# FNet with a squared-ReLU layer, first sequence: other places for the sums of w_out, another engine for the column's folds, pieces repacked

## The chip, the cores and the metric

The kernel runs on one core of a Trainium2 chip. The metric is the device time of one execution in microseconds (us); the median of three runs of the kernel before is 1900.97 us (1900.57 to 1902.41). The engines are called PE (TensorE), DVE (VectorE), ACT (ScalarE), POOL (GpSimd) and SP (SyncE, which here only issues DMAs). Each engine works through its own list of instructions in order, and waits on semaphores for the others.

## The reference

Eight sequences of 3008 rows by 256 columns go through a two-dimensional Fourier transform, of which the real part is kept; the 24064 rows that come out go through two dense layers with a squared ReLU between them.

```python
X = np.fft.fft(x, axis=1)
X = np.fft.fft(X, axis=2)
attn_out = X.real                      # (8, 3008, 256), float32
h = attn_out.reshape(24064, 256) @ w_in      # w_in (256, 2048)
out = np.maximum(h, 0.0) ** 2 @ w_out        # w_out (2048, 256)
```

## The kernel before

**Data.** Everything is fp32. The transform along the rows is done with tables of cosines and sines after the rows of a sequence have been folded onto each other; its two results, `Pt` and `Qt`, hold half of the frequencies of one sequence. The transform along the columns is merged into w_in, which gives `G1` and `G2`.

**Steps.** A sequence b has 6 blocks of up to 252 frequencies, and each block 8 steps j (two slices of 128 of the 2048 hidden features each), so 48 steps for a sequence and 384 in all, numbered i. A step begins with its front (L975): products `hP` and `hQ` into two PSUM buffers, then on DVE `he` (two instructions, L988) and `g` (L990, L991); then ACT does ReLU and square on `g` (L995, L998) and POOL the sums `s` (L1010 to L1012 in even steps, L1020 to L1027 in odd ones). The products with w_out are made for two steps together, with fewer products than usual, from sums of `g` and sums of blocks of w_out (`wsum`): an odd step i does `first_half` (12 products F) for steps i-3 and i-2, the even step after it `second_half` (8 products S). After the fourth pair of a block, `gather` adds the results up: `upper`, `lower`, `joins`, with j = 2 and 3 of the next block. Only the first block (steps 0 to 7) uses `plain` products (L1067, four of 504 columns for a step), since `wsum` isn't there yet.

**Order.** It is written out by hand. Up to step 9 the fronts are cut into halves ("f8b" is the product of the second half of front 8, "d8b" its DVE part), and a list of names, ORDER (L1342), gives the order of everything: conversion of the weights (TS, PW, H, PR), "rl" and "sq" for ReLU and square, "bk6" for the plain products of step 6, "sum8" for the sums of w_out, "fe" and "gE" for a small product and its copy. From step 10 (PLAIN) a loop (L1460) sets the order.

**Sums of w_out.** `sum_wout` (L374) handles one of four groups of SUMS for one half of the columns: ACT copies one or two blocks of w_out into a PSUM buffer, DVE makes 3 to 6 sums or differences from the copy and a block in SBUF, some of them in place. `sums_at` spreads the eight calls over steps 8 to 14. A plain product of a step must come before its slice of w_out is overwritten.

**Pieces.** While one sequence goes through its steps, the next one is folded and transformed, in pieces beside the steps. `fold_later` (L571) makes them: R(t) adds and subtracts the rows of a tile t (ACT copy into PSUM, then DVE `fs` and `fd`, L584 and L585), C(t) folds its columns (two ACT copies into PSUM, two DVE instructions `sc`), `both` splits parities, `order` reverses rows, `even`, `odd` and `twice_...` are later stages. The tiles are called 0, 1, TWO, TWO+1, av, aw, bv, bw. `dft_ops` (L686) makes the pieces "beside", whose products stand between those with w_out: `even` and `odd`, 8 for a sequence. The first sequence has 4 more for one column of all later sequences; that column comes in through small DMAs into `xe` (`load_column`), ACT doubles it (`scale_columns`), and `fold_columns` (L454) folds it in some 20 tiny instructions. `part_table` rearranges tables on ACT.

`ahead(b)` (L1178) puts the pieces of sequence b in line, each with a weight in us. `pieces` (L1320) takes up to two at each step while a budget allows; `piece_beside` is run between the second and the third product. Steps with j = 2 and 3 have hardly a share (SHARE, FIRST).

**Buffers.** The scratch of R, C and the others (`spare`) and of the pieces "beside" comes from the same two PSUM buffers, tag "h", as `hP` and `hQ`: what reads a scratch holds back a front. A buffer freed first is given out first. The two PSUM buffers "d" hold `S1`, `S2` and the small products "pe". `xt`, a tile of x, has three SBUF buffers: R(t) of one tile issues the load of the tile three places later in LATER (L185).

Of the kernel before, what the change touches and what calls it, by code (L numbers as in the profile page):

```python
# [15 lines left out]
P = 128  # L16
R = 32
# [67 lines left out]
def kernel(  # L85
# [99 lines left out]
    LATER = [(b, t) for b in range(1, B) for t in (TWO, TWO + 1, 0, *range(ODD0, NL), 1)]  # L185
# [188 lines left out]
    def sum_wout(qs, shared):  # L374

        ps, held = spare(slice(0, P)), {}
        for i, d in enumerate(shared):
            held[d] = ps[:, i * D:(i + 1) * D].rearrange("p (q h) -> p q h", q=2)  # L380
            nc.scalar.copy(held[d], A(*d)[:, qs])
        for u, v, op, to in SUMS[shared]:
# [71 lines left out]
    def fold_columns():  # L454
# [12 lines left out]
        def begin():  # L467
            s = hp.tile([P, 2, NL, NE], F32, name="es", tag="es", bufs=1)
            tt(out=s, in0=xe[:, 0::2], in1=xe[:, 1::2], op=ALU.add)
            for kp in range(2):  # L470
                tt(out=we[:, :, kp], in0=s[:, 0], in1=s[:, 1], op=ALU.subtract if kp else ALU.add)
# [5 lines left out]
        def copy_even():  # L477
            nc.scalar.copy(a, we[r, first, 0])

        def even():  # L480
            butterfly(we[r, first, 0], we[r, other, 0], a)

        def odd():
            for i, u in enumerate((other, first)):
                tt(out=m[:, 3 * i:3 * i + 3], in0=we[r, u, 1], in1=turned(SIN + i, u), op=ALU.mult)
            for u in (first, other):
                tt(out=we[r, u, 1], in0=we[r, u, 1], in1=turned(COS, u), op=ALU.mult)
            tt(out=we[r, both, 1], in0=we[r, both, 1], in1=m, op=ALU.add)

        def copy_pairs():  # L490
# [3 lines left out]
            nc.scalar.copy(pair, we[r, v, 1])  # L494

        def twice_even():
            butterfly(we[r, 2:3, 0], we[r, 4:5, 0], one)
            for i, u in enumerate((5, 7)):
                mix(out=we[r, u, 0], in0=we[r, u, 0], scalar=by(BY_AB, COS), in1=f[:, i], op0=ALU.mult, op1=ALU.add)

        def twice_odd():
            butterfly(we[r, v, 1], we[r, w, 1], pair)

        return [(0.8, begin), (0.3, order), (0.0, copy_even), (1.0, odd), (0.5, even), (0.0, copy_pairs),
                (0.9, twice_even), (0.5, twice_odd)]
# [65 lines left out]
    def fold_later(b):  # L571
# [5 lines left out]
        def rows_of(t):  # L577
            r = rows(t)

            def f():  # L580
# [4 lines left out]
                tt(out=fd[t][r], in0=v[r, 0::3], in1=p, op=SUB)  # L585
                load_later(LATER.index((b, t)) + NX)

            return 1.3, f
# [89 lines left out]
        R, C, both = rows_of, columns_of, parities_of  # L678
        one = [R(TWO), R(TWO + 1), C(TWO), R(0), C(TWO + 1), both(TWO, TWO + 1), R(av), C(0), order(TWO + 1), C(av),
# [6 lines left out]
    def dft_ops(b):  # L686
# [8 lines left out]
        def group(kp, which):  # L695
# [86 lines left out]
            def join_2():  # L782
                a, ps = st["b"], st["ps"]
                st["c"] = held_w() if both_in else hp.tile([P, NC[0][3]], F32, name="dc2", tag="dc2", bufs=2)[0:n, 0:n0]
# [274 lines left out]
    def second_half(q, n, s, hook=None):  # L1059

        if q == 0:
            open_banks(("S0", "S1", "S2"))
        run((("S0", 0, 8, s[:, 2]), ("S0", 1, (0, 1), s[:, 4]), ("S0", 2, (0, 2), s[:, 8]), ("S1", 0, (1, 0), s[:, 6]),
             ("S1", 1, 11, s[:, 10]), ("S2", 0, 7, s[:, 7]), ("S2", 1, (1, 3), s[:, 5]), ("S1", 2, 10, s[:, 3])),
# [113 lines left out]
    def ahead(b):  # L1178
        (_, start), *groups = dft_ops(b)
        tables = [(0.0, lambda tab=tab, t=t: part_table(tab, t)) for t in (TWO, ODD0) for tab in (cosT, sinT)]  # L1180
        if b == 1:
            early = [(0.0, start), (0.0, take_turn), (0.5, make_turn)]
            middle = [(0.0, scale_columns)] + fold_columns() + tables + dft_ops(None)
        else:
            early, middle = [], []
            groups = [(0.0, start)] + groups
        one, two = fold_later(b)
        return early + one + middle + two + groups
# [120 lines left out]
    FIRST = (1.6, 2.6, 0.2, 0.2, 0.9, 1.9, 1.6, 1.9)  # L1309

    ROOM = (1.6, 2.4, 0.0, 0.0, 1.0, 1.8, 1.6, 1.8)
# [3 lines left out]

    def free_pieces():
        while side and not side[0][0]:
            side.pop(0)[1]()

    def pieces():  # L1320
# [3 lines left out]
        room, count = ROOM[i % NJ] if i >= per else 2.8, 2  # L1324
        while side and count:
            t, f = side[0]
            if f in beside or not t or t > room or spent + t / 2 > 0:
                return
# [248 lines left out]
```

## Time and profile before

| What | Value |
|---|---|
| Median of three runs | 1900.97 us |
| The profiled execution, its own time | 1901.05 us |
| Its span, first to last instruction | 1899.3 us |
| Granted clock of PE, mean | 0.997 |
| PE busy | 1868.8 us, 98% of the span |
| DVE busy | 1478.6 us, 78% |
| POOL busy | 1450.8 us, 76% |
| ACT busy | 1083.0 us, 57% |
| Chain of waits | PE 86%, DVE 10%, ACT 2% |

The page's shares are means over the whole. The first sequence takes the first 302.58 us (the front of step 48 begins then), the next ones some 227 us each; 1.75 us lie outside the span. The idle time of an engine in the groups of instructions stands behind the bar, with what ended it.

### The profile page before, as it was taken

The page shows a single profiled execution, that of the slowest core. Times are in us where ns is not written, and L with a number is a line of the kernel's source. Part 1 is how long each engine was busy: PE and PEld are TensorE (multiplying, and loading weights), DVE is VectorE, ACT ScalarE, POOL GpSimd, SP SyncE. Part 2 cuts the span into 40 slices and gives each one's busy share as a digit, 9 for nine tenths or more (in the row PEclk, how much of TensorE's full clock was granted, in tenths as well). Part 3 has the DMA queues.
Part 4 walks back from the last instruction along what each step waited for, and adds up shares of the span by engine and source line. Part 5 has one row for each costly group of instructions (what it writes and reads, how often), then busy time and mean ns, then how long its engine had stood idle before and what let it go on. Part 6 is the DMA issues. An engine that isn't in the chain of part 4 may idle for free.

```text
span 1899.3 us, 34013 instructions
## 1 busy us (share of the span) xinstructions
PE 1868.8 (98%) x11408; PEld 1755.3 (92%) x11408; DVE 1478.6 (78%) x3507; ACT 1083.0 (57%) x1612; POOL 1450.8 (76%) x2115
## 2 busy tenths in 40 slices
PE   9999999999999999999999999999999999999998
PEld 7678889999999999999999999999999999999997
DVE  8688877888778877888778887788877888766665
ACT  5865655666456654656555574566645656445453
POOL 4367667887788887878778887788778878787886
PEclk9999999999999999999999999999999999999999
DMA  6431101110011000111011110111001100000000
GB/s 196 116 43 32 40 14 42 48 34 15 20 45 51 23 20 20 51 40 29 23 32 31 45 31 15 32 45 48 15 15 45 39 14 19 16 22 15 20 20 23
DMA packets 151310, 68.46 MB, mean 36 GB/s; under 512 B 131143, under 2 KB 142881, under 8 KB 151136
## 3 DMA queue, kind: packets, MB, share of 16 engines
q1 hardware_dynamic: 150590, 65.74, 13.8%
q8 instruction: 91, 1.49, 0.3%
q14 instruction: 83, 0.68, 0.1%
q0 software_dynamic: 416, 0.43, 0.1%
q10 hardware_dynamic: 130, 0.12, 0.0%
HBM read 41.54 MB, written 24.69 MB: 35 GB/s over the span
## 4 chain that ended last, share of the span: by engine, by line
PE 86%; DVE 10%; ACT 2%; issue 1%; POOL 0%; DMA 0%; SPq 0%; DVEq 0%; ACTq 0%; POOLq 0%
PE F L1045 31%; PE S L1045 19%; PE hP L984 15%; PE hQ L984 15%; DVE he L988 2%; PE pd L837 1%; PE pd L714 1%; DVE g L990 1%; DVE g L991 1%; PE mA L1074 1%; PE mB L1074 1%; PE pd L811 1%; PE pg L344 1%; ACT sp L644 1%; PE ph L955 0%
## 5 line engine op out<-in xcount | busy, mean ns | idle before, releaser
L995 ACT ACTIVATE g<-g 128x1008 f32<-128x1008 f32 (+1 forms) x384 | 399.4, 1040 | 313.7 <-DVE g L991 306.0
L988 DVE SCALAR_TENSOR_TENSOR he<-ew,gE,hP 128x252 f32<-128x252 f32 (+1 forms) x748 | 321.2, 470 | 295.9 <-PE hP L984 295.7
L998 ACT ACTIVATE g<-g 128x1008 f32<-128x1008 f32 (+1 forms) x384 | 399.3, 1040 | 12.0
L984 PE MATMUL hP<-Pt,G 128*128 128x252 f32 (+1 forms) x1496 | 380.1, 377 | 8.0 <-DVE w L646 2.9
L984 PE MATMUL hQ<-Qt,G 128*128 128x252 f32 (+3 forms) x1496 | 380.3, 377 | 5.0 <-DVE Pt L749 1.0
L1045 PE MATMUL F<-s,wsum 128*128 128x168 f32 (+1 forms) x1504 | 337.5, 306 | 0.0
L1020 POOL TENSOR_TENSOR s<-g 128x168 f32<-128x168 f32 (+1 forms) x188 | 101.8, 542 | 299.0 <-ACT g L998 294.6
L984 PEld LDWEIGHTS hQ<-Qt,G 128*128 128x128 f32 (+1 forms) x1496 | 280.2, 190 | 48.1 <-ACT g L995 4.2
L1045 PE MATMUL S<-s,wsum 128*128 128x168 f32 (+1 forms) x1504 | 305.7, 305 | 0.0
L1045 PE MATMUL F<-g,wout 128*128 128x168 f32 (+1 forms) x1504 | 305.7, 305 | 0.0
L984 PEld LDWEIGHTS hP<-Pt,G 128*128 128x128 f32 x1496 | 265.2, 190 | 29.7 <-ACT sp L631 4.3
L990 DVE TENSOR_TENSOR g<-he,hQ 128x504 f32<-128x504 f32 (+1 forms) x374 | 253.2, 677 | 49.8 <-PE hQ L984 6.2
L1045 PE MATMUL S<-s,wout 128*128 128x168 f32 (+1 forms) x1504 | 281.2, 306 | 0.1
L1045 PE MATMUL F<-g,wsum 128*128 128x168 f32 (+1 forms) x1504 | 275.0, 305 | 0.0
L1045 PEld LDWEIGHTS S<-s,wsum 128*128 128x128 f32 x1504 | 249.5, 190 | 8.2
L991 DVE TENSOR_TENSOR g<-he,hQ 128x504 f32<-128x504 f32 (+1 forms) x374 | 250.5, 670 | 0.0
L1045 PEld LDWEIGHTS F<-s,wsum 128*128 128x128 f32 x1504 | 248.8, 190 | 0.3 <-issue 0.2
L1045 PEld LDWEIGHTS F<-g,wsum 128*128 128x128 f32 x1504 | 240.6, 190 | 8.1
L1045 PEld LDWEIGHTS F<-g,wout 128*128 128x128 f32 x1504 | 240.6, 190 | 0.0
L1045 PEld LDWEIGHTS S<-s,wout 128*128 128x128 f32 x1504 | 232.1, 190 | 0.7 <-POOL s L1027 0.3
L1026 POOL TENSOR_TENSOR s<-s 128x336 f32<-128x336 f32 (+1 forms) x188 | 168.6, 897 | 14.7
L1023 POOL TENSOR_TENSOR s<-s 128x336 f32<-128x336 f32 (+1 forms) x188 | 168.5, 896 | 14.7
(227 smaller groups left out, 2498.5 us busy)
## 6 DMA issues: line engine op xcount, KB each, us to landing
out_dram<-os SPq DMA_DIRECT2D x376, 56.0 KB
xt<-in_x_dram SPq DMA_DIRECT2D x39, 384.0 KB
xt<-in_x_dram SPq DMA_DIRECT2D x63, 128.0 KB
ew<-e_dram SPq DMA_DIRECT2D x39, 126.0 KB
out_dram<-os SPq DMA_DIRECT2D x288, 7.0 KB
raw<-in_moe_w_in_dram SPq DMA_DIRECT2D x16, 256.0 KB
raw<-in_moe_w_out_dram SPq DMA_DIRECT2D x16, 256.0 KB
xt<-in_x_dram SPq DMA_DIRECT2D x2, 512.0 KB
```

Of the source, the lines that this page charges most:

```text
L344: nc.tensor.matmul(pg, tab[:, i], win[j][:, i], start=i == 0, stop=i == 1)
L984: nc.tensor.matmul(to[:, h, 0:n], w[:, fs], v[:, ks], start=h == 0, stop=True, skip_group_check=True)
L988: nc.vector.scalar_tensor_tensor(out=t[:, h, 0:n], in0=window[b, k0][:, 0:n], scalar=gE[:, fc:fc + 1], in1=hP[:, h, 0:n], op0=ALU.mult, op ...
L990: tt(out=g[:, :, 0:n], in0=t[:, :, 0:n], in1=hQ[:, :, 0:n], op=ALU.add)
L991: tt(out=g[:, :, n:2 * n][:, :, ::-1], in0=t[:, :, 0:n], in1=hQ[:, :, 0:n], op=ALU.subtract)
L995: act(g[:, :, 0:2 * n], g[:, :, 0:2 * n], AF.Relu)
L998: act(g[:, :, 0:2 * n], g[:, :, 0:2 * n], AF.Square)
L1020: gt(out=s[:, 11], in0=b2[:, 0], in1=b1[:, 0], op=SUB)
L1023: gt(out=s[:, 4:6], in0=s[:, 4:6], in1=s[:, 10:11].to_broadcast([P, 2, tb]), op=SUB)
L1026: gt(out=s[:, 6:9:2], in0=s[:, 2:4], in1=s[:, 6:8], op=ADD)
L1045: nc.tensor.matmul(acc[nm][:, slot, 0:tb], w, v, start=q == 0 and nm not in begun, stop=q == NJ // 2 - 1, skip_group_check=True)
L1074: nc.tensor.matmul(acc[nm][:, 0:2 * n], wout[:, j, h, c], g[:, c, 0:2 * n], start=j == c == 0, stop=j == NJ - 1 and c == 1)
```

## The change

1. ORDER is new from "sq4" on. The sums of w_out are no longer one item: "sc" copies a group on ACT into a PSUM buffer "d" (before: "h"), "su" does the DVE part. Groups of the first half (a) stand among steps 4 to 8, those of the second half (b) in steps 8 to 11.
2. The plain products bk6 stand between fronts 8 and 9 (before: behind both halves of front 9), bk7 stands before front 10 (before: behind it).
3. In the first sequence `fd` of R(t) is made on POOL from SBUF; its weight goes from 1.3 to 0.7.
4. The folds of the column go from DVE to POOL, with weights of about 0.1, and are woven between other pieces; multiply-adds are split in two.
5. The pieces of the first sequence have another order (R(1) is the fourth R, where it was the last) and another packer, `first_pieces`, with a room for each j and none for j = 2 and 3. A piece "beside" can now share a step with a piece that holds a scratch. Tile 1 is loaded fourth instead of last.
6. In `second_half` the third product of S1 comes ahead of the two of S2, in all sequences.

```diff
-    LATER = [(b, t) for b in range(1, B) for t in (TWO, TWO + 1, 0, *range(ODD0, NL), 1)]
+    LATER = [(b, t) for b in range(1, B)
+             for t in (TWO, TWO + 1, 0, *(() if b > 1 else (1,)), *range(ODD0, NL), *((1,) if b > 1 else ()))]
...
-    def sum_wout(qs, shared):
-        ps, held = spare(slice(0, P)), {}
-        for i, d in enumerate(shared):
+    shared_w = {}
+    def copy_wout(k, h):
+        ps, held, qs = psd.tile([P, 2 * D], F32, name="sw", tag="d"), {}, slice(2 * h, 2 * h + 2)
+        for i, d in enumerate(list(SUMS)[k]):
             held[d] = ps[:, i * D:(i + 1) * D].rearrange("p (q h) -> p q h", q=2)
             nc.scalar.copy(held[d], A(*d)[:, qs])
-        for u, v, op, to in SUMS[shared]:
+        shared_w[k, h] = held
+    def sum_wout(k, h):
+        held, qs = shared_w.pop((k, h)), slice(2 * h, 2 * h + 2)
+        for u, v, op, to in list(SUMS.values())[k]:
...
         def begin():
+            scale_columns()
             s = hp.tile([P, 2, NL, NE], F32, name="es", tag="es", bufs=1)
-            tt(out=s, in0=xe[:, 0::2], in1=xe[:, 1::2], op=ALU.add)
+            gt(out=s, in0=xe[:, 0::2], in1=xe[:, 1::2], op=ADD)
...
-        return [(0.8, begin), (0.3, order), (0.0, copy_even), (1.0, odd), (0.5, even), (0.0, copy_pairs),
-                (0.9, twice_even), (0.5, twice_odd)]
+        return [(0.1, begin), (0.3, order), (0.1, odd), (0.1, even), (0.1, odd_sums), (0.1, twice_even), (0.1, twice_odd)]
...
-                tt(out=fd[t][r], in0=v[r, 0::3], in1=p, op=SUB)
+                if b == 1:
+                    gt(out=fd[t][r], in0=v[r, 0::3], in1=v[r, 1:3], op=SUB)
+                else:
+                    tt(out=fd[t][r], in0=v[r, 0::3], in1=p, op=SUB)
...
+        if b == 1:
+            one = [R(TWO), R(TWO + 1), C(TWO), R(0), C(TWO + 1), both(TWO, TWO + 1), R(1), C(0), order(TWO + 1), C(1),
+                   R(av), both(0, 1), even((TWO, TWO + 1)), odd(TWO, TWO + 1, BY_TWO)]
+            two = [C(av), R(aw), R(bv), C(aw), both(av, aw), C(bv), order(aw), R(bw), even((av, aw)), odd(av, aw, BY_AC),
+                   C(bw), both(bv, bw), order(bv), even((bv, bw)), odd(bv, bw, BY_BD)]
...
-             ("S1", 1, 11, s[:, 10]), ("S2", 0, 7, s[:, 7]), ("S2", 1, (1, 3), s[:, 5]), ("S1", 2, 10, s[:, 3])),
+             ("S1", 1, 11, s[:, 10]), ("S1", 2, 10, s[:, 3]), ("S2", 0, 7, s[:, 7]), ("S2", 1, (1, 3), s[:, 5])),
...
+        head = [(0.0, start), (0.2, take_turn), (0.5, make_turn)] + one[:9]
+        return (head + woven(one[9:] + two[:3], fold_columns(), 1) + tables
+                + woven(two[3:], dft_ops(None) + groups[0::2], 1) + groups[1::2])
...
+    CAPACITY = (1.8, 2.9, 0.0, 0.0, 1.2, 2.2, 1.8, 2.2)
+    def first_pieces(j):
+        nonlocal spent
+        room, hook = CAPACITY[j], None
+        while side:
+            t, f = side[0]
+            if spent + t / 2 > 0 or t > room + (0.6 if f in beside else 0.3) or f in beside and (hook or late):
+                break
+            side.pop(0)
+            if not t:
+                late.append(f)
+                continue
+            spent, room = spent + t, room - t
+            if f in beside:
+                hook = (2, f)
+            else:
+                f()
+        return hook
...
-        'gE6 PRw4 d6b sq5 fe7 pgC7 gE7 TSw5 bk4 TSw6 PWw5 restQ GC7 d6a spl PWw6 Hw5 f7b PRw5 f7a TSw7 bk5 Hw6 '
-        'PWw7 d7b PRw6 rl6 d7a sq6 f8b Hw7 f8a rl7 d8a sq7 PRw7 d8b sum8 rl8 f9a sq8 hi8 f9b d9a cm8 bk6 '
-        'd9b rl9 sum9 sq9 hi9 cm9 '
+        'gE5 PRw3 pgD6 d5b sq3 f5a GC6 H7 bk3 GD6 rl4 TSw4 PR7 PWw4 d5a pgD7 restP rl5 fe6 Hw4 f6b GD7 sq4 sc0a f6a '
+        'su0a gE6 PRw4 d6b sq5 fe7 pgC7 gE7 TSw5 bk4 TSw6 PWw5 restQ GC7 d6a spl PWw6 Hw5 f7b sc1a PRw5 f7a su1a TSw7 '
+        'bk5 Hw6 PWw7 d7b PRw6 rl6 d7a sq6 f8b Hw7 sc2a f8a rl7 su2a d8b sq7 PRw7 d8a sc3a sc1b bk6 rl8 su3a hi8 su1b '
+        'f9a sq8 f9b d9a cm8 sc2b d9b sc0b rl9 hi9 su2b sq9 bk7 cm9 '
...
-            if i < NJ + 7:
-                sums_at(i)
+            if i == PLAIN:
+                sum_wout(0, 1)
+                copy_wout(3, 1)
+            elif i == PLAIN + 1:
+                sum_wout(3, 1)
...
-        if i == PLAIN:
-            back_at(NJ - 1)
-        elif at >= NJ and at < len(steps):
+        if at >= NJ and at < len(steps):
```

## The prediction

> **What bounds the kernel now.** I read the page's busy shares first, then each engine's busy time by stretches, then what PE waited for, then PE's timeline where it idles.
>
> ```profile
> PE 1868.8 (98%) x11408; PEld 1755.3 (92%) x11408; DVE 1478.6 (78%) x3507; ACT 1083.0 (57%) x1612; POOL 1450.8 (76%) x2115
> ```
>
> PE is the bound over the span, so only PE's idle, slow or waiting time can be won. Stretches (length, then busy time of PE, weight loads, DVE, ACT, POOL) tell where it lies:
>
> ```profile
> 115.13:132.62 17.49, 15.58 (x90) 13.54 (x90) 16.14 (x40) 12.26 (x24) 12.11 (x19) 1.00 0.48 73
> 176.30:225.69 49.39, 45.96 (x283) 41.35 (x282) 41.43 (x101) 29.00 (x50) 34.09 (x50) 1.00 0.17 42
> 302.58:529.39 226.81, 226.18 (x1410) 216.07 (x1409) 181.96 (x428) 131.12 (x194) 180.44 (x264) 1.00 0.12 32
> ```
>
> The second sequence (last row) has PE full; the first has not, and between fronts 13 and 16 (first row) DVE is busier than PE. In steady steps the fronts are 5.12 us (odd) and 3.98 us (even) apart in the timeline; a piece "beside" adds 0.75. From front 10 (100.12) to front 48 (302.58) that makes 172.9, less 0.6 for the six shorter fronts, plus 12 x 0.75: 181.3 of 202.5 us. 21 us are lost there, some 0.14 a piece of it unavoidable, as in the second sequence. Who held PE:
>
> ```profile
> PE hP L984 <- DVE fd L585: 1.9, 4, 0.8
> PE hP L984 <- DVE w L615: 1.9, 1, 1.9
> PE hP L984 <- DVE sc L600: 0.9, 1, 0.9
> ```
>
> DVE's pieces, reading a scratch in a PSUM buffer that the next front needs. Ahead of front 10:
>
> ```profile
> 90.98 0.69 PE L955 MATMUL ph<-Pt,G 128*128 128x252 f32 x2 [2.63 <-DVE g L973]
> 92.97 1.21 PE L955 MATMUL ph<-Pt,G 128*128 128x252 f32 x2 [0.76 <-DVE wout L384]
> 96.50 1.88 PE L1074 MATMUL mB<-g,wout 128*128 128x504 f32 x2
> 99.28 1.01 PE L1074 MATMUL mB<-g,wout 128*128 128x504 f32 x2
> ...
> 92.00:94.00 2.00, 1.24 (x4) 0.86 (x4) 1.97 (x6) 1.11 (x2) 0.78 (x1) 0.50 0.36 3
> ```
>
> Two gaps, 3.4 us, and behind the first the granted clock is 0.50 to 98.7, so the same product takes 1.88 instead of 1.01: another 2.9. So about 27 us, 1.4%, are there to be won, all before 303 us.
>
> **Part by part, against the profiled execution's 1901.05** (the median of the runs shown is 0.08 lower). Work of PE is only moved.
>
> *1. ORDER, sums and plain products (73 to 115 us).* bk6 (four products, 3.4) fills the gap ahead of front 9: 3.4 and the 2.9 of slow clock could come back. But DVE pays. Thirteen more of the sums (0.41 each, starting 0.34 apart: 4.4 us) stand ahead of front 10, and they wait for ACT, whose copies (0.37) queue behind sq4 (ends 76.07) and the conversions. So su0a runs from 76.9 to 79.0 where DVE had idled; the small product fe7 now needs su0a's PSUM buffer (the order of instructions with their waits shows it) and goes from 76.7 to 79.0, with PE's queue behind it: 2.3 lost. su1a waits for sc1a behind a conversion (2.1) on ACT: TSw7 moves from 82.7 to about 87.3, and with it front 8 from 86.5 to 89.7. bk6 then ends at 95.4, bk7 at 100.5, front 10 begins there (before: 100.12), but bk7's 3.4 no longer follow. DVE enters front 10 at 103.0 (before 101.2), with 9 sums to come instead of 22. Carried on: front 13 at 113.5 instead of 115.13. **Gain 1.6.**
>
> *2. Fewer DVE pieces (fronts 13 to 16).* DVE's instructions in these steps go from 6.2, 5.7, 4.8 to 4.4, 3.8, 4.6 (`fd` gone: eight of 0.677 in all; the last sums gone). PE then loses 1.3 instead of 3.3: **gain 2.0**, front 16 at 129.0 instead of 132.62. POOL pays for `fd`: the row at L1209 is the same operation on the same x tile, 1.30 us. Hidden in POOL's waits for squares (L1020: 39.5 us in 16 waits), one in two steps.
>
> *3. Loads (16 to 19).* R(1) moves from step 32 to step 15. Its tile's load is issued on SP behind the `xe` DMAs, which take SP 0.44 to 0.5 each: before, the first load behind them left at 128.2, and such a load landed at 131.3 to 131.9. SP's queue is hardly earlier now (its stores still wait for `os`, 112.3 instead of 112.7). So ACT's copy in R(1), wanted at 127, waits to about 131, with relu and square of front 15 behind it, and `hQ` of front 16 (free when `fs` is done, 132.6) comes 2.75 late. Then scale_columns, moved from step 21 to 17, waits on ACT for the last `xe` DMA (about 141; 0.95). **Loss 3.1.** Without it R(1) would cost nothing.
>
> *4. POOL's lag (19 to 25).* A pair of steps lasts 9.1 and POOL's sums take 8.0 of it. Steps 13 to 23 add seven `fd` (9.1) and the column's fifteen instructions. POOL has no row for those; its smallest of this kind are 0.54 (128x168) and 0.41 (the shorter L1213), its memsets 0.10, DVE's on these shapes 0.16 uncontended: 2.4 to 8.1 us, not below nothing, since they are added to POOL. I take 3.5 (0.23 each, nearest by size). With it `fd` of aw comes at about 171, and the copy that C(aw) wants at 167 waits on ACT; behind it stand a ReLU, a square and the tables, for which a product "beside" waits 0.9. Front 24 loses 1.65. Before, 1.8 were lost here: **loss 0.9**; front 25 at 176.6 instead of 176.3.
>
> The folds leave DVE: 6.2 us by their rows, in steps 21 to 23, where DVE wasn't the bound, so they count nothing beyond that. Two of them, 56 elements wide, took 583 and 816 ns where 7 to 14 elements take 161 to 172. The Trainium skill (SBUF — State Buffer, Who interferes with whom) says that a VectorE instruction with two SBUF inputs contends with a GpSimd instruction that reads SBUF; these rows agree. By that rule POOL's prices are the short ones and the sum would be about 1 us better; new waits of `fd` on DVE are not to be expected, since DVE's other operands here come one from PSUM.
>
> *5. The rest (25 to 48).* Before: 13.4 lost, 2.1 to 2.3 at each gather with pieces (DVE 7.9 to 8.8 us in steps 26, 34, 42, against 6.2 in the second sequence, where nothing is lost). The new packer puts none there: 6.2. But in steps 25, 32, 33 and 41 a piece with a scratch precedes one "beside", which then gets the front's second buffer and waits for `g` instead of `he`: at +3.2 us instead of +2.27, so 0.95 each, 1.5 in step 41, where DVE is behind. Before, all twelve waited for `he` alone. With 11 x 0.14, 0.8 at step 40 (two pieces in 3.98 us) and 0.45 for the rest: 7.1. **Gain 6.3.**
>
> *6. S1 ahead of S2.* Only the end sees it: L1113 starts at 1890.11, after the last product (1890.0), and L1114 0.53 later; now L1113 is done by then. **Gain 0.5.** In other steps DVE arrives there after PE.
>
> Sum: 1.6 + 2.0 - 3.1 - 0.9 + 6.3 + 0.5 = 6.4, so **1894.6**. Cover that can go: if SP's stores were late by 2 us more, term 3 grows by the same.
>
> **Rivals.**
>
> *Loads and POOL keep up.* SP idled from 110.6 to 112.7 for the stores; if `os` comes early, the tile lands before 129 and R(1) waits little; with POOL's short prices C(aw) doesn't wait. Terms 3 and 4 vanish: 1894.6 - 3.1 - 2.6 = 1889, and 1885 if the gaps of the prologue come back as well. For it: DVE's sums of durations overstate (instructions overlap by 0.08). Against: the `xe` DMAs' pace is a row. Chance 0.27.
>
> *The clock drops.* The wait of 2.75 at front 16, or the 2.3 at fe7, could do what the gap of 2.63 did: half clock for 6.8 us, 2.9 to 3.4 each. 1898. A gap of 1.93 at 229.8 did not, so the limit is between. The Trainium skill (TensorE: Matmul & The Clock Gate, What's actually happening) gives an idle window of about 3.4 us for the drop; by that rule neither gap would do it and this case is void, but here 2.63 idle us sufficed. Chance 0.13.
>
> *Slower: POOL becomes the bound through ACT.* At 0.54 per column instruction POOL is 8.1 - 3.5 = 4.6 further behind; from about 3 us on, ACT's steps of the column (step 22) and C's copies wait for POOL at once, with ReLU and square behind them, so POOL's own input is late too. 4.6, and two waits long enough to halve the clock, 3.4 each, on 1894.6: 1906. For it: seven `fd` and 15 instructions in 50 us that have 6 free. Against: POOL waited 39.5 us for squares. Chance 0.12.
>
> *It doesn't do what it says.* DVE's relief is eaten by the four waits for `g` and by ACT (as long in each), so terms 2 and 5 halve: 1899. Chance 0.06.
>
> **Numbers.** Forecast 0.42, its own range 1890 to 1898. About 0.2% (3.8 us) is what a measurement of this kernel can tell from no change: faster means below 1897.2, slower above 1904.8. Faster: forecast 0.38, first rival 0.27, clock 0.06: 0.71. Same: 0.04 + 0.07 + 0.06 + 0.02 = 0.19 with the slow case's lower part. Slower 0.10. The range 1885 to 1902 leaves out most of the slow case and the best of the first.
>
> **What will show it.** Term 1: PE waits at the product `pe` near 77 for `wout`, no 0.50 clock near 92, front 13 near 113.5. Term 2: no `fd` on DVE in the first sequence, 1.3 each on POOL. Term 3: ACT's `sp<-xt` near 127 released by a DMA; `hQ` of front 16 by `fs`. Term 4: `sp<-fd` waiting for POOL. Term 5: gather steps as in the second sequence, `pd` waiting for `g` four times; front 48 near 296.6. It is wrong if the later sequences change from 227 us, or if PE's clock drops in the first.

## The result, and the profile after

The changed kernel takes 1903.71 us (median of 20 runs, 1902.52 to 1906.55), the kernel before 1900.51 (20 runs, 1899.98 to 1902.41). The ratio is 1.0019, with a 95% interval of 1.0012 to 1.0026: a little slower. The forecast was 1894.6.

Work was moved, as announced: the page of the changed kernel, to be held against that of before, has PE's busy time to the tenth as it was, 9 us less on DVE, 12 more on POOL.

```profile
PE 1868.8 (98%) x11408; PEld 1757.6 (92%) x11408; DVE 1469.8 (77%) x3483; ACT 1082.4 (57%) x1614; POOL 1463.2 (77%) x2138
```

The fronts tell where the time went. Gains are against the kernel before, from the starts of `hP` in the two timelines:

| Front | before | after | forecast | gain |
|---|---|---|---|---|
| 10 | 100.12 | 100.07 | 100.5 | 0.05 |
| 13 | 115.13 | 112.01 | 113.5 | 3.12 |
| 16 | 132.62 | 129.74 | 129.0 | 2.88 |
| 17 | 137.18 | 140.83 | | -3.65 |
| 25 | 176.30 | 179.77 | 176.6 | -3.47 |
| 48 | 302.58 | 304.12 | 296.6 | -1.54 |
| end of the span | 1899.3 | 1901.3 | | -2.0 |

One step, 16, loses 6.5 us against the kernel before, and steps 25 to 47 win 1.9 where 6.3 were forecast. The stretches of the changed kernel (length, then busy time of PE, weight loads, DVE, ACT, POOL, granted clock) are the fronts 13 to 16, then 16 to 19, 25 to 34, and the second sequence:

```profile
112.01:129.74 17.73, 15.10 (x90) 13.45 (x89) 12.79 (x30) 10.32 (x20) 15.72 (x22) 1.00 0.33 32
129.74:149.94 20.20, 15.69 (x83) 14.58 (x82) 10.55 (x25) 10.65 (x17) 15.64 (x23) 0.83 0.54 106
179.77:231.03 51.26, 47.06 (x299) 43.46 (x298) 39.06 (x99) 28.93 (x49) 37.31 (x55) 1.00 0.15 33
304.12:531.24 227.12, 226.33 (x1410) 216.07 (x1409) 182.03 (x428) 131.07 (x194) 180.39 (x264) 1.00 0.13 32
```

In the first row DVE (12.79) is no longer the fullest engine, so that part of the change did its work. In the second, each of PE, DVE, ACT and POOL is idle for 4 us and more of 20, and the clock is 0.83: the bound is none of them. PE's waits between 70 and 305 us name the instructions that released it:

```profile
PE hQ L1002 <- DVE fs L593: 4.5, 1, 4.5
PE hQ L1002 <- DVE sc L612: 2.9, 2, 2.6
PE pe L356 <- DVE gE L360: 2.1, 1, 2.1
PE pd L732 <- DVE g L1009: 2.0, 2, 1.0
PE pd L855 <- DVE g L1009: 1.7, 2, 0.9
PE hQ L1002 <- DVE dc L785: 1.3, 1, 1.3
```

DVE stands behind every arrow, but in the first two lines it was not DVE that was late. In ACT's timeline the copies that feed `sc` and `fs` show what held them: a `fd` on POOL in step 14 and the load of tile 1 in step 15.

```profile
119.90 0.37 ACT L609 COPY sp<-fd 96x254 f32<-96x254 f32 x1 [2.87 <-POOL fd L595]
...
133.81 0.58 ACT L591 COPY sp<-xt 94x512 f32<-94x512 f32 x1 [6.40 <-DMA xt<-in_x_dram]
```

And SP's timeline (start, time to issue, count) shows where the load had been: behind 12 of the 56 small DMAs into `xe`.

```profile
123.50 5.70 SPq L454 DMA_DIRECT2D xe<-in_x_dram  x12
129.30 0.38 SPq L183 DMA_DIRECT2D xt<-in_x_dram  x1
129.79 0.36 SPq L174 DMA_DIRECT2D xt<-in_x_dram  x1
130.20 7.07 SPq L454 DMA_DIRECT2D xe<-in_x_dram  x12
```

The load of tile 1 left at 129.30, ACT copied from 133.81 on. PE then ran what followed at half clock: in its timeline the four products of `hQ` behind the wait take 2.02, the four of `hP` ahead of it 1.01.

```profile
129.74 1.01 PE L1002 MATMUL hP<-Pt,G 128*128 128x252 f32 x4
135.26 2.02 PE L1002 MATMUL hQ<-Qt,G 127*128 127x252 f32 x4 [4.51 <-DVE fs L593]
```

Ahead of the last microseconds of the span, the records of the granted clock have 0.5 from 133.23 for 6.83 us, and from 78.62 for 3.41 us, behind the wait of `pe`. In the kernel before there was one such stretch, 6.83 us from 91.86.

### The profile page after: what moved, and what is told of

The parts are those of the page before. It is cut to its first block, busy times and chain, and to the rows that moved or that the text cites. A ratio compares the mean times of both kernels' runs of the same rounds, so it can differ in the third digit from the quotient of the medians.

```text
span 1901.3 us, 34082 instructions
## 1 busy us (share of the span) xinstructions
PE 1868.8 (98%) x11408; PEld 1757.6 (92%) x11408; DVE 1469.8 (77%) x3483; ACT 1082.4 (57%) x1614; POOL 1463.2 (77%) x2138
## 4 chain that ended last, share of the span: by engine, by line
PE 82%; DVE 11%; ACT 2%; POOL 2%; issue 1%; DMA 0%; DVEq 0%; ACTq 0%; POOLq 0%
PE F L1063 29%; PE S L1063 19%; PE hP L1002 15%; PE hQ L1002 14%; DVE he L1006 2%; PE pd L732 2%; PE pd L855 1%; DVE g L1008 1%; DVE g L1009 1%; PE pd L829 1%; ACT sp L656 1%; PE pg L345 0%; DVE vt L1132 0%; ACT g L1016 0%; ACT g L1013 0%
## 5 line engine op out<-in xcount | busy, mean ns | idle before, releaser
L1063 PE MATMUL S<-s,wsum 128*128 128x168 f32 (+1 forms) x1504 | 275.7, 306 | 0.0
L1063 PEld LDWEIGHTS S<-s,wsum 128*128 128x128 f32 x1504 | 241.2, 191 | 8.3 <-issue 0.2
```

What stands on the lines that cost most here:

```text
L1063: nc.tensor.matmul(acc[nm][:, slot, 0:tb], w, v, start=q == 0 and nm not in begun, stop=q == NJ // 2 - 1, skip_group_check=True)
```

## The experiments

The theory after this reading: the small DMAs into `xe` on SP set the time at which x tiles arrive, and with it the time of front 17, whatever is won ahead of it; the other losses are the named waits. The main rival: DVE, ACT or POOL is the bound in the first sequence, and what is taken away at one wait comes back at the next. Times below are medians, ratios are to the kernel before, run beside. "Loses" means the length of a step beyond its products at full clock.

**e1: tile 1 ahead of the small DMAs** (from the changed kernel).

```diff
-            if i < COLUMNS:
-                load_column(i - NJ)
...
                 hook = (2, piece_beside)
+        if PLAIN <= i < COLUMNS:
+            load_column(i - NJ)
```

> The changed kernel, but in each step from 10 on the small DMAs into xe are issued behind the step's pieces instead of ahead of them, so that the load of tile 1 (issued by R(TWO) in step 12) leaves SP ahead of the 12 DMAs that took it from 123.50 to 129.24 in the changed kernel. Nothing else moves on PE, DVE, ACT or POOL. Theory (step 16's 7.10 us are the load's 4.5 us of waiting and what the half clock from 133.2 on costs, and the load alone causes both): step 16 loses at most 0.5, no half clock near 133, 6.6 us less than the changed kernel, about 1897. Rival (R(1) is late for fd on GpSimd or for the third xt buffer, and the load only hides that): the load still lands after 129 or fs still comes late, 2 us less or nothing, 1901.5 to 1904. Second rival (ACT and DVE are behind in this stretch anyway, so steps 17 to 24 lose what step 16 wins): about 1900.

Measured: 1907.41, ratio 1.0033 (1.0020 to 1.0045), 3.7 us worse than the changed kernel. Step 16 lost nothing, as the theory had it, but step 18 lost 9.0, and step 14, where the same wait of 2.6 was now followed by half clock, 4.55 instead of 2.91. ACT's longest wait in this run:

```profile
ACT xe L458 <- DMA xe<-in_x_dram: 8.7, 1, 8.7
```

The wait only moved: `scale_columns`, which the change had brought from step 21 to 17, wants the last small DMA, and that was now later. (The small DMAs are 56 instructions in SP's trace, 34 us of issuing; the 90 in a later expectation is a slip.) Neither theory nor rival had named this one, though the prediction had, with 0.95 us.

**e2: a shared piece beside put later** (from the changed kernel).

```diff
-                hook = (2, f)
+                hook = ((6 if j % 2 else 5) if ran else 2, f)
             else:
                 f()
+                ran = True
```

> The changed kernel, but in the first sequence a piece beside that shares its step with another piece is put between the sixth and seventh product (odd steps) or the fifth and sixth (even steps) instead of between the second and third; alone it stays where it is. No work changes. Theory (pd waits for g, 3.7 us in 4 waits, because the scratch took the first of the two PSUM buffers): by then g is done, about 3.2 us less than the changed kernel, 1900.5, and no wait of pd for g over 0.3 us. Rival (DVE is behind in these steps, so the piece's later products only push dc to the next front): hQ waits for dc instead, by 0.7 to 1.5 us in as many steps, 1903 to 1905.

Measured: 1901.72, ratio 1.0001 (0.9993 to 1.0010). Only half of the edit took effect: in steps 32 and 33 the other piece is called behind the line that sets the place, so those two waits stayed (1.41 and 1.38 lost, as before). In steps 25 and 41 the loss fell by 0.94 and 1.10, to 1.72 and 1.25. So the two waits of `pd` are real and go away without coming back as `dc`: the wait of 1.3 for `dc` in step 25 stands ahead of the piece and is the same in both kernels.

**e3: the eight `fd` back on DVE** (from the changed kernel).

```diff
-                if b == 1:
+                if b == 0:
                     gt(out=fd[t][r], in0=v[r, 0::3], in1=v[r, 1:3], op=SUB)
```

> The changed kernel with the eight fd of the first sequence back on DVE (0.677 each, 5.4 us in all), weights and packing as changed, so that only the engine differs. Theory from the trace of the changed kernel (C(TWO)'s copy in step 14 waited 2.9 us for fd, which stood behind sums on GpSimd): step 14 loses 2.2 less; DVE has 4.4 to 5.1 us of work in a step of 5.12 and takes the rest without loss except in steps 13 and 15 (0.3 each): about 1.5 less, 1902. The prediction's term 2 the other way round: 2.0 lost, about 1905.7, with hP waiting for fd on DVE by 1.9 in four waits as in the kernel before.

Measured: 1904.56, ratio 1.0020 (1.0011 to 1.0029): against the changed kernel's 1.0019 nothing that can be told apart. Fronts 13 to 16 took 16.4 us instead of 17.7, but step 16 then lost 9.75 instead of 7.10: front 16 came 1.0 earlier, but the load of tile 1 left SP at 129.95 instead of 129.30, so front 16 waited longer. The experiment can't size `fd`, and that is its result: what is won ahead of front 16 is lost in it. It was repeated as e15 with the loads out of the way.

**e4: gE6 ahead of su0a** (from the changed kernel).

```diff
-... sq4 sc0a f6a su0a gE6 PRw4 ...
+... sq4 sc0a f6a gE6 su0a PRw4 ...
```

> The changed kernel with one swap in ORDER: gE6 ahead of su0a, so that the small product fe7 finds its PSUM buffer free at once. Theory (PE is without a gap from 78.4 to 100 in the changed kernel, so that the stall of 2.1 us at 76 and the half clock of 3.4 us behind it are passed on whole): front 10 starts 3 to 3.7 us earlier, and the time falls by as much, to 1900.3. Rival (DVE, which ends its sums at 101.4 in front 10, becomes the bound, so fronts 10 to 13 lose it): front 10 earlier by 3, front 13 by 1 at most, time 1902.7 to 1903.7.

Measured: 1903.29, ratio 1.0009 (1.0000 to 1.0018). The wait of 2.1 and the half clock behind it are gone, but front 10 came 0.95 earlier and front 11 only 0.2: `hP` waits 1.1 for `he` on DVE, which also has the last sums of w_out to make. The time is the rival's, though neither text had front 10 right (3 us earlier).

**e5: e1, and the column's folds three pieces later.**

```diff
-        return (head + woven(one[9:] + two[:3], fold_columns(), 1) + tables
+        return (head + one[9:12] + woven(one[12:] + two[:3], fold_columns(), (1, 1, 1, 2, 2)) + tables
```

> The first experiment (tile 1 loaded ahead of the small DMAs) with the column's folds, scale_columns among them, three pieces later in the line, so that the ACT instruction that wants the last small DMA is not reached before step 20 or so. Theory (the trace of the first experiment: step 16 lost nothing, but ACT waited 8.7 us for xe at scale_columns and step 18 lost 9.0; SP's 90 small DMAs at 0.49 us are what both wait for): no step from 16 to 24 loses over 0.8, front 19 starts at 145 instead of 149.9, the time is 5 us below the changed kernel's, 1898.7. Rival (GpSimd, with fd and the column's instructions, is late by the same amount, and the loads hide it): C(av) or C(aw) waits for fd, front 25 no earlier than 178, time 1901 or more.

Measured: 1904.55, ratio 1.0018 (1.0009 to 1.0027). Up to front 23 the theory held: no step from 16 to 22 lost over 0.7, front 19 began at 143.88, front 23 at 162.24 instead of 168.81. Then step 23 lost 10.1. ACT's and PE's waits there:

```profile
ACT xe L502 <- POOL we L485: 5.8, 1, 5.8
PE pd L829 <- ACT cosT L427: 5.9, 1, 5.9
```

Two folds to a piece put `twice_even`, whose copy is on ACT, right behind the even folds on POOL, which stood behind sums and a `fd`; ReLU, square and the tables queued behind the copy, and a product waited 5.9 for a table. The experiment's packing made this wait, but it is the mechanism of the prediction's slower rival, POOL through ACT.

**e6: e5 with `fd` of TWO on DVE, e4's swap, and e2's edit for all four steps.**

```diff
-                if b == 1:
+                if b == 1 and not (t == TWO):
...
-                hook = (2, f)
+                hook = f
             else:
                 f()
-        return hook
+                alone = False
+        return hook and (2 if alone else 6 if j % 2 else 5, hook)
```

> The experiment before it (loads and scale) with three more edits: fd of tile TWO alone on DVE (C(TWO)'s copy in step 14 had waited 2.9 us for it on GpSimd), gE6 ahead of su0a, and a piece beside that shares its step put behind the fourth product or later, in steps 25, 32, 33 and 41 alike. Theory (the named waits are all there is): against that experiment step 14 wins 3.5 (2.6 of waiting and what the half clock behind it costs), the prologue 0.9, the four waits of pd 3.6: 8 us, so 1890 to 1892. Rival (DVE is behind in steps 13 to 16 and 24 to 41, what goes at one wait comes back at the next): half of it, 1894.7 or more.

Measured: 1901.89, ratio 1.0006 (0.9998 to 1.0015). Front 16 now began at 127.36, and step 16 lost 5.0: tile 1 left SP at 125.16, behind the stores and four small DMAs, and ACT waited 4.9 for it, up to 129.97. Step 23 lost 8.9 as in e5. The other edits did what was said: step 14 lost 0.16 instead of 2.91, steps 25 and 33 lost 0.20 and 0.24 instead of the 1.26 and 1.38 of e5 (steps 32 and 41 had lost 0.15 and 0.50 in e5 already).

**e7: the kernel before with the new ORDER alone** (items sc and su, and the plain products' places; the loop's sums as in the change).

```diff
-... Hw4 f6b GD7 sq4 f6a gE6 ... d8b sum8 rl8 f9a sq8 hi8 f9b d9a cm8 bk6 d9b rl9 sum9 sq9 hi9 cm9
+... Hw4 f6b GD7 sq4 sc0a f6a su0a gE6 ... sc3a sc1b bk6 rl8 su3a hi8 su1b f9a sq8 f9b d9a cm8 sc2b d9b sc0b rl9 hi9 su2b sq9 bk7 cm9
...
-        if i == PLAIN:
-            back_at(NJ - 1)
-        elif at >= NJ and at < len(steps):
+        if at >= NJ and at < len(steps):
```

> The kernel before with the new ORDER and the sums of w_out as separate items alone (and the plain products between the half fronts): fd and the column's folds on DVE, pieces, weights, loads and the order of S as before. The prediction's term 1: 1.6 us, 1898.9. Theory from the trace of the changed kernel (front 13 came 3.1 earlier): 3 us, 1897.5, if fronts 13 to 16 pass it on, since there is no load to wait for (R(1) is in step 32). Rival (DVE is the bound in steps 13 to 16, and the earlier fronts wait for the same fd): front 17 no earlier than 136.5, 1900 to 1900.8.

Measured: 1902.67, ratio 1.0008 (0.9999 to 1.0017). No gain, but for no reason that was expected. Fronts 13 to 16 passed the gain on and added to it: front 16 began at 127.89, 4.7 us earlier than in the kernel before. Then steps 16 and 17 lost 6.0 where they had lost 0.7. SP's timeline, first that of the kernel before and then this run's, and ACT's copy of the tile:

```profile
122.34 5.75 SPq L448 DMA_DIRECT2D xe<-in_x_dram  x12
128.20 1.77 SPq L174 DMA_DIRECT2D xt<-in_x_dram  x4
```

```profile
123.95 6.05 SPq L453 DMA_DIRECT2D xe<-in_x_dram  x12
130.11 1.77 SPq L174 DMA_DIRECT2D xt<-in_x_dram  x4
```

```profile
134.11 0.59 ACT L587 COPY sp<-xt 96x512 f32<-96x512 f32 x1 [4.79 <-DMA xt<-in_x_dram]
```

In this kernel R(1) is the last R and `scale_columns` is in step 21: nothing of the change's pieces is in it. The tile of av waits behind the small DMAs, which leave no earlier than before, though front 16 comes 4.7 earlier: the tile left at 128.2 in the kernel before, at 130.1 here.

**e8: S1 ahead of S2 alone** (from the kernel before).

```diff
-             ("S1", 1, 11, s[:, 10]), ("S2", 0, 7, s[:, 7]), ("S2", 1, (1, 3), s[:, 5]), ("S1", 2, 10, s[:, 3])),
+             ("S1", 1, 11, s[:, 10]), ("S1", 2, 10, s[:, 3]), ("S2", 0, 7, s[:, 7]), ("S2", 1, (1, 3), s[:, 5])),
```

> The kernel before with one edit: the third product of S1 ahead of the two of S2, in all sequences. The prediction's term 6: 0.5 us less, at the end alone, 1900.0. Theory from the traces (steps 36 and 44 of the later sequences are 0.07 longer each in the changed kernel, 1.0 us over seven sequences, and the end is 0.8 shorter): no difference, 1900.5 within 0.3, with those steps 0.07 longer. Rival (those 0.07 are from another edit): 1899.7, steps 36 and 44 as before.

Measured: 1902.12 (1900.35 to 1904.32), ratio 1.0004 (0.9995 to 1.0013): no gain, and a loss can't be told from none. Step 36 lost 0.63 instead of 0.56, step 43 2.39 instead of 2.31, and the start of sequence 8 moved from a gain of 0.15 (front 48) to a loss of 1.16. That this is the edit shows in the other profiles: from front 48 to the front of step 336 (sequences 2 to 7) the five kernels without it take 1360.95 to 1361.78 us, the thirteen with it 1362.77 to 1363.54. So the edit costs these sequences some 1.3 us. The fastest version below (e13) still has it; without it no such kernel was run.

**e9: e7 with the small DMAs behind the pieces** (e1's edit).

> The kernel with the new ORDER alone, and its small DMAs into xe issued behind the pieces of each step from 10 on instead of ahead of them; scale_columns is in step 21 there. Theory (with the ORDER alone front 16 began 4.7 us earlier than in the kernel before, and ACT then waited 4.8 us for the x tile that left SP at 130.1 behind 12 small DMAs; steps 16 and 17 lost 6.0 in place of 0.7, so that front 18 came no earlier: the small DMAs set the time of front 17, whatever is won ahead of it): with the tile's load ahead of them steps 16 and 17 lose at most 1.5 together, front 19 begins by 142.5 instead of 147.0, and the time is 4 to 5 us below that of the ORDER alone, about 1898. Rival (DVE, with fd and C in these steps, is the bound anyway): hP waits for fd or sc for as long, front 19 at 145.5 or later, 1901 or more.

Measured: 1897.47, ratio 0.9981 (0.9972 to 0.9989). Steps 16 and 17 lost 0.7 together, front 19 began at 141.70, 5.3 us before e7's. One edit to the order in SP's queue makes the difference of 0.27% between the two ratios. The tile now left at 126.18:

```profile
126.18 1.93 SPq L174 DMA_DIRECT2D xt<-in_x_dram  x4
128.15 5.03 SPq L453 DMA_DIRECT2D xe<-in_x_dram  x10
```

**e10: e9 with e4's swap.**

> The same with gE6 ahead of su0a in ORDER, so that fe7 doesn't wait 2.1 us for its PSUM buffer. Theory: fronts 10 to 19 come 0.5 to 1 earlier than in the same without the swap, and the time falls by as much, 1897.3. Rival (DVE's sums end at the same time, so front 11 begins no earlier): no difference within 0.3.

Measured: 1897.20, ratio 0.9979 (0.9970 to 0.9987). Fronts 11 to 48 came 0.2 us earlier: the rival again.

**e11: the changed kernel with all small DMAs six steps later, the column's folds and products later in the line.**

```diff
-            if i < COLUMNS:
-                load_column(i - NJ)
...
+        if 14 <= i < 14 + NL:
+            load_column(i - 14)
...
-        return (head + woven(one[9:] + two[:3], fold_columns(), 1) + tables
-                + woven(two[3:], dft_ops(None) + groups[0::2], 1) + groups[1::2])
+        fold, left = fold_columns(), groups[0::2]
+        others = left[:1] + fold[:2] + left[1:2] + fold[2:] + dft_ops(None) + left[2:]
+        return head + one[9:] + two[:3] + tables + woven(two[3:], others, 1) + groups[1::2]
```

> The changed kernel with all small DMAs into xe six steps later (steps 14 to 21, behind the pieces), and the column's folds and products later in the line, scale_columns at step 24 or later, so that neither an x tile nor scale_columns waits for them. Theory (they are what steps 16 or 18 wait for in every kernel so far): no step from 16 to 24 loses over 0.8, front 19 at 143 to 145 instead of 149.9; step 14 keeps its loss of 2.9 or 4.5 (fd on GpSimd), the four waits of pd stay: 1898 to 1899. Rival (GpSimd's queue of fd, sums and folds is the bound behind the loads, as in the experiment with the folds three pieces later, where ACT waited 5.8 us for it): a wait of over 2 us for GpSimd somewhere in steps 20 to 32, 1901 or more.

Measured: 1899.63, ratio 0.9995 (0.9986 to 1.0004), 4.1 us less than the changed kernel. Step 16 lost 0.0, no step from 16 to 23 over 0.6, front 19 began at 144.58. Step 14 kept its 2.91; step 31 lost 3.4, with GpSimd behind it (see e12): the rival's part is there as well.

**e12: e11 with e6's other edits.**

> The same with fd of TWO on DVE, gE6 ahead of su0a and the shared pieces beside put later. Theory (all named waits gone): step 14 wins 3.5, the prologue 0.9, the waits of pd 3: 7 us below the same without them, 1891 to 1892, and below the kernel before by 9. Rival (another bound comes up at once, DVE in steps 13 to 16): 1895 or more.

Measured: 1892.94, ratio 0.9956 (0.9943 to 0.9970), 8.1 below the kernel before. One long wait was left, in step 31, which lost 5.1 (a wait of 3.0, then half clock). That wait of PE and ACT's behind it:

```profile
PE hQ L1002 <- DVE w L627: 3.0, 1, 3.0
ACT xe L502 <- POOL we L485: 2.6, 1, 2.6
```

**e13: e12 with the even folds five places ahead of `twice_even`.**

```diff
-        others = left[:1] + fold[:2] + left[1:2] + fold[2:] + dft_ops(None) + left[2:]
+        others = left[:1] + fold[:2] + left[1:2] + fold[3:4] + fold[2:3] + left[2:3] + fold[4:] + dft_ops(None) + left[3:]
```

> The experiment with the small DMAs late and all named waits removed, with the column's even folds five places ahead of twice_even instead of right ahead of it. Theory (the 5.1 us that step 31 loses there are ACT's copy in twice_even, which waits 2.6 us for the even folds on GpSimd with step 30's ReLU and both()'s copies behind it, and the half clock that follows): step 31 loses under 1, no half clock before the end, 4 to 5 us less, 1888.5. Rival (GpSimd is simply behind in these steps, and the copy waits wherever it is put): a wait of over 2 us in steps 28 to 33, 1891 or more.

Measured: 1887.95, ratio 0.9932 (0.9920 to 0.9945): 12.5 us below the kernel before, and the fastest version. Step 31 lost nothing, the clock stays at 1.00 up to the end, front 48 begins at 288.10. What PE still waits for:

```profile
PE ph L973 <- ACT G L350: 1.3, 1, 1.3
PE hP L1002 <- DVE he L1006: 1.1, 1, 1.1
PE hQ L1002 <- DVE dc L785: 0.8, 1, 0.8
```

**e14: the kernel before with the small DMAs behind the pieces** (e1's edit alone).

> The kernel before with one edit: from step 10 on the small DMAs into xe behind the pieces of a step instead of ahead of them. Theory (in the kernel before, DVE sets fronts 13 to 17, and the x tile that left SP at 128.2 came just in time): no difference, 1900.5 within 0.6, front 17 at 137 as before. Rival (the loads bound the kernel before as well): front 17 earlier by 1 or more, 1899 or less.

Measured: 1899.37, ratio 0.9993 (0.9984 to 1.0002). Steps 13 to 17 lost what they lose in the kernel before, to the hundredth. In the kernel before the queue was no bound; it was the next one. The 1.1 us can't be told from nothing. In the profiled execution front 10 began at 97.52, 2.6 earlier, since the half clock ahead of it lasted 3.4 instead of 6.8 us; step 35 lost 1.7 more, behind another half clock.

**e15: e13 with all `fd` of the first sequence on DVE** (e3's edit; the "first kernel" of the expectations is e13, here and in the next).

> The first kernel of this call with all eight fd of the first sequence on DVE. The prediction's term 2: 2.0 us lost in fronts 13 to 16. Theory (with the sums of w_out gone from steps 13 to 15, DVE has 3.8 to 5.1 us of work there and takes 0.68 more without much loss): 0.5 to 1 slower, in step 13 above all, 1889 to 1889.5. Rival (fd on GpSimd costs more than it saves, through C's copies on ACT): 0.5 faster or more.

Measured: 1889.80, 1.85 above e13; ratio 0.9941 (0.9929 to 0.9954). That is more than the theory's 0.5 to 1 and against the rival; 0.9 of it lies in fronts 13 to 16, the rest in the steps up to front 25. PE waits for `fd` on DVE again:

```profile
PE hP L1002 <- DVE fd L597: 2.9, 4, 1.0
```

**e16: e13 with the column's folds on DVE** (`gt` to `tt` in `fold_columns`).

> The first kernel of this call with the column's folds on DVE (some 20 instructions of 0.16 us, the wide ones 0.6 to 0.8), ACT's part and the packing as they are. The prediction's term 4: GpSimd's lag through the folds costs 0.9, so that the time falls by about that. Theory (0.2 to 0.57 each on GpSimd, 6 us over ten steps, behind sums): 0 to 1 faster, ACT's waits for we gone. Rival (DVE is fuller than GpSimd in these steps): 1 us slower or more.

Measured: 1891.87, 3.9 above e13; ratio 0.9956 (0.9942 to 0.9969). The rival's reading: DVE was busy for 7.0 us in step 29 in place of 5.3, and steps 25, 29 and 30 lost 4.4 instead of 0.6. The tile `we`'s instructions in e16 and then in e13 (minimum, median, maximum in ns) show the same operation on the two engines:

```profile
L494 DVE TENSOR_TENSOR xe<-we,turn x2: 571/814/1057, 196.7 to 197.7; 94x21 f32<-94x21 f32 x2
```

```profile
L494 POOL TENSOR_TENSOR xe<-we,turn x2: 218/218/218, 198.3 to 198.5; 94x21 f32<-94x21 f32 x2
```

While DVE made these two in e16, POOL had a `fd` and a sum in work, with operands in SBUF:

```profile
195.58 1.27 POOL L595 TENSOR_TENSOR fd<-xt 96x512 f32<-96x512 f32 x1
196.82 0.90 POOL L1028 TENSOR_TENSOR s<-g 128x336 f32<-128x336 f32 x1
196.70 1.55 DVE L494 TENSOR_TENSOR xe<-we,turn 94x21 f32<-94x21 f32 x2
```

The packing is e13's, whose weights of 0.1 were made for folds on POOL; a packing that leaves DVE room for them was not run.

## Why the prediction was wrong, point by point

**Where the 8.5 us went.** The forecast was 6.4 faster, the profiled span is 2.1 longer. Of the difference, 0.7 is missing at front 16 (terms 1 and 2), 2.4 between fronts 16 and 25 (terms 3 and 4), 4.4 between fronts 25 and 48 (term 5) and 1.0 behind front 48 (term 6). The step that turned a gain into a loss is term 3, and the largest sum is missing in term 5.

**The step that failed first is term 3**, "Loss 3.1". Its place and its line were right: ACT's copy waited for a DMA, `hQ` of front 16 for `fs`. Its size was 6.5 in step 16 alone. The tile was to be there at about 131, and came at 133.81. Of that, 1.1 are the queue: the load left at 129.30 for 128.2, since SP, which had idled from 110.6 to 112.7 in the kernel before, now issued small DMAs up to 113.6 and its stores behind them. The rest is the way: ACT had the tile 4.5 us after the issue, where the prediction had taken 3.1 to 3.7. No wait of a run shows these: where ACT waits for such a tile of 384 KB, it has it 4.0 (e7), 4.3 (e9), 4.6 (e3) and 4.8 us (e6) after the issue. So the wait was 4.5 instead of 2.75. The half clock behind it added 2.6 (step 16 lost 7.1 in all, 0.6 before), which the sum had put at nothing and a rival at a chance of 0.13. The small wait for `scale_columns` (0.95) didn't come: step 17 lost nothing.

What the sum does not show is that the gains ahead of this load are worth nothing. Term 3 had been worked out for a front 16 at 129.0, and would have been larger for an earlier one, since the load does not move with the front: with front 16 at 129.74, 128.71 (e3) and 127.89 (e7) the tile behind the small DMAs left at 129.30, 129.95 and 130.11. e7 won 4.7 by front 16 and lost 5.3 in the next two steps, e3 won 1.0 and lost 2.7. With the copy at 133.81, `hQ` at 135.26 and 3.1 us of products behind it at full clock, front 17 of the changed kernel could not begin before some 138, whoever was early. The kernel before had little room: its tile left at 128.20 and was copied at 134.57, which with 4.0 to 4.8 us of way leaves an estimated 1.6 to 2.4.

**Term 1** (1.6) was too small: front 13 came 3.1 earlier, and 2.7 in e7. The wait at `pe` was 2.1 for 2.3, though for `gE`, which stands behind su0a on DVE, and not for `wout`; front 10 came at 100.07 for 100.5, and steps 10 to 12, with DVE's nine sums to come, lost 1.1, where a front 13 at 113.5 stood for 2.2 (13.0 less 10.8 of products). With the loads out of the way (e9) the new ORDER and the loads' edit gain 3.6 us together; the loads' edit alone gave 1.1, not told from nothing (e14).

**Term 2** (2.0) was near in size: e15 against e13 gives 1.85. But only 0.9 of that lies in fronts 13 to 16, where the term had put all of it, so the nearness is in part luck. And "hidden in POOL's waits" failed at one place. `fd` of TWO stood on POOL behind the sums of steps 11 and 12, C(TWO)'s copy waited 2.87 for it, and step 14 lost 2.91, so that front 16 came at 129.74 for 129.0. The lag had been looked for in steps 19 to 25, where POOL is fullest, not at the first use of the first `fd`.

**Term 4** (-0.9) was too dark. POOL's 15 instructions took 3.6 us in e13 (forecast 3.5), and fronts 17 to 25 gained 0.2, though behind a wait in step 16 that gave POOL time, so this is no clean test; in e13, without that wait and with later folds, they lost 0.3. The move that "counts nothing" on DVE is worth 3.9 in e16, with e13's packing. The prediction had quoted the reason, two folds of 583 and 816 ns where others take 161 to 172, and the Trainium skill (SBUF — State Buffer, Who interferes with whom), by which a VectorE instruction with two SBUF inputs contends with a GpSimd instruction that reads SBUF. e16 agrees with it, with 571 and 1057 ns for 21 elements that POOL does in 218. The rule was used for POOL's price, when it spoke about DVE's.

**Term 5** (6.3) was worth 1.9. The part on gathers was right: steps 26, 27, 28, 34, 42 and 43 lost 7.7 before and under 0.1 after. The four waits of `pd` for `g` came where they were announced, 0.9 to 1.0 each, but the four steps lost 7.8, not 4.35. In two of them the front itself had waited before its piece came, which the prediction had at nothing: 1.3 for `dc` in step 25, and 0.4 and 0.8 for `w` in step 41.

```profile
182.07 1.09 PE L1002 MATMUL hQ<-Qt,G 127*128 127x252 f32 x4 [1.29 <-DVE dc L785]
184.61 0.65 PE L855 MATMUL pd<-cosT,we 94*7 94x95 f32 x6 [0.88 <-DVE g L1009]
```

Some 0.4 a step stay without a named wait. Step 40 lost 1.4 for 0.8, the other steps 2.3 for 2.0. The waits of `pd` go when the piece is put three or four products later: step 25 lost 0.94 less in e2, and 0.24 in e12 where e11 had lost 1.39; step 33 lost 0.54 instead of 1.26 there.

**Term 6** (0.5) had the wrong sign. "Only the end sees it" failed: sequences 2 to 7 lose 1.3 (e8). The last sequence and the end took 234.38 us instead of 235.13, but over all kernels the ranges with and without the edit overlap there.

**The rivals.** "The clock drops" happened, at both places that it named, for 3.41 and 6.83 us. "Slower, POOL through ACT" cost the changed kernel only what step 14 lost (term 2), but its mechanism made the longest waits of e5, e6 and e12. "Loads and POOL keep up" is what e13 brought about by other means. That e13's 1888 is near its 1889 is luck: the rival's sum takes away 2.6 for a term 4 of 0.9 (with 0.9 it gives 1890.6), and e13 wins 9.1 in fronts 25 to 48, where term 5 had 6.3.

## What to carry to other kernels

A transfer that is "just in time" is the next bound: before a gain is counted, ask of each load in the stretch when it leaves its queue and whether that time moves with the gain; if it doesn't, the gain ends there, and the terms must not be added but compared. An edit that is made in every sequence for the sake of the end must be read in the later sequences too. When every engine is idle in a stretch, read the queue that issues the DMAs, not the engine behind the arrow, and follow one waiting instruction back through ACT's in-order queue. And when work goes to an engine with room, look at the first consumer of its first result, not at the mean load.

## What the runs showed of the hardware

*The clock goes by a grid.* In the records of the granted clock of all 18 profiles every stretch at half clock before the end is 3.41, 6.83 or 10.24 us long, and those at full clock between them are multiples of 3.413 too (51.2, 37.55, 85.33). The same stall need not do the same: the 2.1 us of `pe` brought half clock in five of the eight profiles that have it and none in three, the 2.6 us in step 14 in three of six. The Trainium skill (TensorE: Matmul & The Clock Gate, What's actually happening) tells of a free-running window of 3413 ns, and the lengths agree with it; its whole idle window of about 3.4 us as the condition for the drop does not: the gap of 1.93 at front 35 did nothing in the kernel before, and the same gap, 1.92, brought 3.41 us of half clock in e14. Nor does a limit between 1.93 and 2.63, as the prediction had it: gaps of 2.1 and 2.6 did it in some profiles and not in others. That the place of the gap in the grid decides is the nearest reading, but was not tried by itself. It is also a likely reason for the spread of the changed kernel's runs, 4.0 us against 2.4.

*Small DMAs cost the queue that issues them*, little as they carry: 12 of 0.9 KB each hold SP for 5.70 us, 0.48 each, and the issue of a tile of 384 KB takes 0.38.

*The same tiny operation on DVE and on POOL* took 152 to 1057 ns on DVE (e16) and 197 to 302 on POOL (e13) at 7 to 56 elements: POOL's was the steadier price.
